# Attention followed by a squared-ReLU feed-forward: single-product weighting of v for the second batch, wider pieces of w_out with their low parts on VectorE, r read later, and the reciprocal moved to the end of its slot

## The chip, the core and the metric

The kernel runs on one core of a Trainium2 chip. The metric is the device time of one execution in microseconds (us), the median of several runs. The engines are TensorE (PE, its weight loads PEld), VectorE (DVE), ScalarE (ACT), GpSimd (POOL) and SyncE (SP), which issues all DMAs here. Each engine takes its instructions strictly in program order, and waits at an instruction until what it needs is there.

## The reference

```python
q_n, k_n = rmsnorm(q, g_q), rmsnorm(k, g_k)          # (8, 12, 448, 64) each
attn = softmax(q_n @ k_n.T / sqrt(64))               # maximum taken off before exp
x = (attn @ v).transpose(0, 2, 1, 3).reshape(3584, 768)
r = np.maximum(x @ w_in, 0.0)                        # w_in (768, 2048)
g = s * (r * r) + b
out = g @ w_out                                      # w_out (2048, 768), out (3584, 768)
```

Inputs are float32, but `w_in` and `w_out` enter with 64 bits per element: the kernel reads them as pairs of 32-bit words and rebuilds a float32 from the words on the chip.

## The kernel before, in words

**Numbers.** A TensorE product in the fast one-pass type (`F32R`) keeps only part of a float32, so a value is split in a high part (an ACT copy to that type) and a low part (what is left, a subtraction), and three products high×high, low×high, high×low stand for one float32 product. The alternative is one product in plain `F32`, which PE runs as two longer instructions.

**Attention (lines 209 to 657).** There are 8 batches of 6 pairs of heads; a pair has 8 slots, one for each head and chunk of 128 keys (`W = 8`), so a batch is 48 slots and there are 384. A loop over slots writes out the order of every engine by hand. In slot `s_` it issues: the transposed scores `st` of slot `s_` (two matmuls, lines 405 and 408), a third of the filler matmuls, the ACT copy `ah` of the exponents of slot `s_-1` (`split_e`), the exponent of slot `s_`, the jobs that a table `jobs` holds for this slot, the scores `sh` of slot `s_+10` for the row maximum (line 367), the low part `al` of slot `s_-1` (`split_e_lo`, line 445, DVE), the maximum (line 378, DVE), the conversion of a piece of `w_in` (`convert`), and the weighting of v for slot `s_-2` (`weigh`, line 464). The jobs of a pair whose first slot is `s0` include: reading v (`load_v`), splitting v in high and low (`split_v`, ACT and POOL), norms and scaling of q and k (DVE line 330, POOL line 329), their low parts (POOL, lines 351 and 352), taking the sums of the softmax out (`gather`, a DMA into `zt`, at `s0+7` and `s0+11`), `divide` step 0 at `s0+13` (add 1e-9 and reciprocal of `zt` on DVE, lines 489 and 490), step 1 (store), step 2 (broadcast load into `zb`) and step 3 at `s0+18` (POOL, line 505, gives `u`). In the slots 11, 12 and 13 of the next batch `split_x` splits the `u` in high and low parts `x` (ACT 513, DVE 514), two pairs in each slot.

In the first batch (pairs `p < NP = 6`) the exponents stay float32 and `weigh` is one float32 product per slot with `vf` (v beside a block of ones, for the sums); from the second batch on, `weigh` is three F32R products (two in every fourth slot, where the low part shares the tile `ah`).

**First matrix of the feed-forward.** From slot 61 on the filler matmuls are `ffn_in` of the batch before (line 180): 16 units of 18 matmuls per batch, 6 per slot. ACT takes each unit's relu out of PSUM (`rectify`, line 197), and SP stores it (`r_d`). Pieces of `w_in` (512 columns, 24 of them) are read and converted in slots -18 to about 94 (`PACE`).

**The row between the matrices (lines 660 to 746, the "w_out row" below).** After attention, the last batch's 16 units of `ffn_in` are left. A loop `m = 0..19` issues a unit (for `m < 16`) and the conversion of three pieces of `w_out` (128 rows × 256 columns, 48 in all): four DVE operations per piece (lines 125, 128, 130, 133), an ACT square (126), and four rounds later an ACT copy to the high part `woh` (136) and a POOL subtraction to the low part `wol` (139), since `woh` and `wol` lie where the quarters of `w_in` lay. The relu of unit `m` stands in round `m` on ACT, between these. In rounds 7 to 12 the squares of the first three tiles of 128 tokens are made (`squares`: ACT 682, DVE 683, then ACT 687 gives `gh`, DVE 688 `gl`); their `r` is read from memory ahead of the loop. The eight PSUM banks are handed out in the order in which they come free.

**Second matrix.** `ffn_out` (line 700): for a tile of 128 tokens 16×3×2 matmuls of 384 columns. The first three tiles share each quarter of `w_out` as it becomes ready; then come tiles 3 to 27, one at a time. These matmuls, and all DMAs of this part, stand in an order that the framework's scheduler chooses.

## Time and profile before

| | us |
|---|---|
| three timed runs | 1546.6, 1547.24 (median), 1549.03 |
| the profiled execution, its device time | 1545.13 |
| its span from the first to the last instruction | 1543.3 |

So 1.8 us of the profiled execution lie outside its span, and it is 2.1 us below the median of the timed runs. In the profile a line such as `L445` is a line of the kernel before; a group's row gives busy time, the mean duration of one, and the idle time of the engine ahead of it with what ended that. A row of the timeline gives start, duration, engine, line, operation, tiles and, in brackets, the wait that ended there; a row of the windows gives each engine's busy time and its count of instructions, the granted clock of TensorE as a share of the full one, and the DMA engines' share. TensorE's durations overlap, so its pace is read from start to start.

### The profile page before, as it was taken

What the parts mean: (1) busy time and instruction counts of PE and PEld (TensorE: products, weight loads), DVE (VectorE), ACT (ScalarE), POOL (GpSimd) and SP (SyncE); (2) the same over time, 40 slices, a digit from 0 to 9 for tenths busy, and PEclk for the clock granted to TensorE, in tenths of its full rate; (3) what the DMA queues carried; (4) which work ended last, traced back from release to release, by engine and by line L of the source; (5) the groups of instructions that cost most, each with busy time, mean ns of one, the idle gap of its engine ahead of it and who ended that gap; (6) DMA issues with size and microseconds to landing.
All of it is one profiled execution on the core that took longest, in us unless ns stands there. A gap on an engine that the chain in (4) does not pass through costs nothing. (4 is left out here: it accounts for less than half of the span.)

```text
span 1543.3 us, 21847 instructions
## 1 busy us (share of the span) xinstructions
PE 1459.3 (95%) x7380; PEld 1343.6 (87%) x7380; DVE 892.6 (58%) x1399; ACT 812.5 (53%) x1522; POOL 748.6 (49%) x611
## 2 busy tenths in 40 slices
PE   7886799999999999999999999997899999999998
PEld 6654688899899899899889889996899999999998
DVE  5989998766666766766666664389532222222210
ACT  4766676666666666766766666346342222222210
POOL 6799898777667667667677753135500000000000
PEclk8998899999999999999999999998899999999999
DMA  4477676566566566656666651466243323323300
GB/s 118 133 198 217 183 231 201 161 193 202 159 189 191 173 193 193 183 166 201 189 172 194 188 164 56 125 218 199 82 140 91 97 75 88 101 76 86 103 21 31
DMA packets 218751, 230.86 MB, mean 150 GB/s; under 512 B 72912, under 2 KB 193744, under 8 KB 218640
## 3 DMA queue, kind: packets, MB, share of 16 engines
q1 hardware_dynamic: 218640, 229.47, 50.3%
q8 instruction: 58, 0.95, 0.3%
q14 instruction: 53, 0.43, 0.1%
HBM read 177.21 MB, written 40.84 MB: 141 GB/s over the span
## 5 line engine op out<-in xcount | busy, mean ns | idle before, releaser
L180 PE MATMUL ph<-x,wih 128*128 128x448 f32 x1536 | 493.1, 368 | 0.0
L424 ACT ACTIVATE st<-st 128x448 f32<-128x448 f32 x336 | 176.5, 525 | 261.2 <-PE st L408 244.6
L180 PEld LDWEIGHTS ph<-x,wih 128*128 128x128 f32 x1536 | 290.8, 189 | 24.0 <-issue 0.2
L378 DVE TENSOR_REDUCE nmx<-sh 112x1 fp32r<-112x448 f32 x384 | 237.1, 620 | 126.4 <-PE sh L367 121.1
L180 PE MATMUL ph<-x,wil 128*128 128x448 f32 x768 | 282.2, 367 | 0.0
L700 PE MATMUL po<-woh,gh 128*128 128x384 f32 x896 | 230.9, 337 | 12.5 <-ACT gh L687 7.8
L700 PE MATMUL po<-wol,gh 128*128 128x384 f32 x896 | 230.5, 337 | 4.1 <-POOL wol L139 4.1
L700 PE MATMUL po<-woh,gl 128*128 128x384 f32 x896 | 229.1, 336 | 0.0
L464 PE MATMUL av<-ah,vs 128*128 128x448 f32 x672 | 194.7, 371 | 6.1 <-DVE ah L445 3.2
L445 DVE TENSOR_TENSOR al<-st,ah 128x448 fp32r<-128x448 f32 x252 | 155.5, 617 | 44.6 <-ACT ah L432 26.0
L432 ACT CAST ah<-st 128x448 fp32r<-128x448 f32 x336 | 179.6, 535 | 2.0
L700 PEld LDWEIGHTS po<-woh,gh 128*128 128x128 f32 x896 | 163.4, 189 | 13.9 <-ACT gh L687 8.1
L367 PE MATMUL sh<-ka,qa 128*112 128x448 f32 x384 | 147.8, 387 | 23.0 <-POOL ka L351 8.4
L700 PEld LDWEIGHTS po<-wol,gh 128*128 128x128 f32 x896 | 163.4, 189 | 5.5 <-POOL wol L139 5.5
L700 PEld LDWEIGHTS po<-woh,gl 128*128 128x128 f32 x896 | 162.9, 189 | 0.5 <-DVE gl L688 0.5
L405 PE MATMUL st<-qa,ka 128*128 128x448 f32 (+1 forms) x384 | 159.2, 414 | 0.5 <-ACT e L420 0.5
L180 PEld LDWEIGHTS ph<-x,wil 128*128 128x128 f32 x768 | 145.2, 189 | 11.4
L351 POOL TENSOR_TENSOR ka<-kq,ka 64x448 fp32r<-64x448 f32 x84 | 100.4, 1196 | 108.4 <-ACT ka L348 97.3
L464 PEld LDWEIGHTS av<-ah,vs 128*128 128x128 f32 x672 | 127.5, 191 | 20.3 <-DVE al L445 3.5
L408 PE MATMUL st<-qb,kb 128*128 128x448 f32 (+1 forms) x384 | 142.4, 371 | 0.0
L682 ACT ACTIVATE r<-r 128x2048 f32<-128x2048 f32 x28 | 53.7, 1917 | 168.2 <-DMA r<-r_d 168.2
L367 PEld LDWEIGHTS sh<-ka,qa 128*112 128x112 f32 x384 | 107.7, 281 | 36.0 <-POOL ka L351 9.9
(75 smaller groups left out, 2099.1 us busy)
## 6 DMA issues: line engine op xcount, KB each, us to landing
kq<-in_dram SPq DMA_DIRECT2D x84, 448.0 KB, 4.8
rb<-i_d SPq DMA_DIRECT2D x84, 448.0 KB, 5.5
r_d<-r SPq DMA_DIRECT2D x128, 224.0 KB, 2.0
r<-r_d SPq DMA_DIRECT2D x24, 1024.0 KB, 5.8
raw<-in_dram SPq DMA_DIRECT2D x42, 448.0 KB, 4.7
w64i<-in_dram SPq DMA_DIRECT2D x24, 512.0 KB, 4.8
w64o<-in_dram SPq DMA_DIRECT2D x48, 256.0 KB, 3.1
kb<-ka SPq DMA_DIRECT2D x96, 112.0 KB, 3.4
```

The source lines that it names most:

```text
L180: T.matmul(ph[:, :SEQ], w[:, cc, f0 : f0 + P], xs[b, cc][:, part, :], start=n == 0, stop=n == 3 * NCC - 1,)
L351: G.tensor_tensor(ka[n][D:, a], t[D:, 0], ka[n][D:, a].bitcast(F32), ALU.subtract)
L367: T.matmul(sh[:QC, :SEQ], qa[p % 2][:, a].rearrange("k (p c) -> k c p", c=NQ)[:, c], ka[p % 2][:, a], start=True, stop=True,)
L378: V.tensor_reduce(out=nmxs[p][:, c : c + 1], in_=sh[:QC, :SEQ], op=ALU.max, axis=AX.X, negate=True)
L405: T.matmul(st[:rows, :SEQ], ka[n][:, keys], qa[n][:, q], start=True, stop=False)
L408: T.matmul(st[:rows, :SEQ], kb[n][:, keys], qb[n][:, q], start=False, stop=True,)
L424: S.activation(st[:rows, :SEQ], st[:rows, :SEQ], AF.Exp)
L432: S.copy(ah[:rows], sts[i][0][:rows, :SEQ])
L445: V.tensor_tensor(al, st[:rows, :SEQ], ah[:rows].bitcast(F32), ALU.subtract)
L464: T.matmul(av[:, :SEQ], x, a, start=kc == 0 and m == 0, stop=kc == 3 and m == len(todo) - 1,)
L682: S.activation(r, r, AF.Square)
L700: T.matmul(po[e][0][:, :HALF], x[:, fc, :], w[:, f, e * HALF : (e + 1) * HALF], start=fc == 0 and m == 0, stop=fc == NFC - 1 and m == 2,)
```

## The change

Four things are changed.

1. `NV = 2 * NP` takes the place of `NP` wherever the choice between one float32 product and three split products is made. Pairs 6 to 11, the second batch, lose `split_v`, `split_e` and `split_e_lo`; their exponent goes to SBUF as float32 on ACT, v is read by two DMAs with two POOL memsets, and `weigh` is one float32 product.
2. `w_out` comes in 32 pieces of 384 columns, two per round `m`, with four buffers for the words from memory (five before), and the low part is subtracted by DVE (`rest=V`), one step after the ACT copy of the high part.
3. The reads of `r` for the first three tiles are issued in rounds 1, 2 and 3 and no longer ahead of the loop, and their squares stand in rounds 6 to 11 (7 to 12 before).
4. The reciprocal of the sums, step 0 of `divide`, is a function of its own, `invert`, which is issued where `convert` is, after the slot's low part and maximum.

```diff
+    NV = 2 * NP
...
-    WO = 256
+    WO = 384
...
-    def load_double(room, dst_hi, dst_lo, src, apart=False):
+    def load_double(room, dst_hi, dst_lo, src, apart=False, rest=None):
...
         S.copy(dst_hi, af)
         if apart:
             yield
-        G.tensor_tensor(dst_lo, af, dst_hi.bitcast(F32), ALU.subtract)
+        (rest or G).tensor_tensor(dst_lo, af, dst_hi.bitcast(F32), ALU.subtract)
...
         def load_v(p):
-            if p < NP:
+            if p < NV:
...
         def exponent(i):
             p, j, kc, rows = chunk(i)
             st, bank = sts[i]
-            if p < NP:
+            if p < NV:
...
         def split_e_lo(i):
             p, j, kc, rows = chunk(i)
-            if p < NP:
+            if p < NV:
                 return
...
+        def invert(p):
+            zt = zts[p]
+            V.tensor_scalar(zt, zt, 1e-9, None, ALU.add)
+            V.reciprocal(zt, zt)
...
+        late = (convert, invert)
...
-            at(s0 - (9 if p >= NP else 5), load_v, p)
-            if p >= NP:
+            at(s0 - (9 if p >= NV else 5), load_v, p)
+            if p >= NV:
                 at(s0 - 3, split_v, p)
-            at(s0 + 13, divide, p, 0)
+            at(s0 + 13, invert, p)
...
                 for f, a in jobs[s_]:
-                    if f is convert:
+                    if f in late:
                         f(*a)
...
-                w = op.tile([P, WO, 2], I32, tag="w64", bufs=5, name=f"w64o{i}")
-                a = op.tile([P, WO], I32, tag="wa", bufs=16, name=f"wao{i}")
-                m = op.tile([P, WO], F32, tag="wm", bufs=3, name=f"wmo{i}")
-                yield load_double((w, lambda a=a: a, m), *part)
+                w = op.tile([P, WO, 2], I32, tag="w64", bufs=4, name=f"w64o{i}")
+                m = op.tile([P, WO], F32, tag="wm", bufs=2, name=f"wmo{i}")
+
+                def words(i=i):
+                    return op.tile([P, WO], I32, tag="wa", bufs=10, name=f"wao{i}")
+
+                yield load_double((w, words, m), *part, apart=True, rest=V)
...
-            todo = list(islice(pieces, 3))
-            for g in chain(todo, first):
+            todo = list(islice(pieces, 2))
+            for g in todo:
                 next(g)
...
+                if m in (1, 2, 3):
+                    next(first[m - 1])
...
-                    if step == 1:
+                    if step == 0:
                         rectify()
                         keep_r()
-                    if step == 2:
                         for g in old:
                             for _ in range(GAP):
                                 next(g)
+                    if step == 2:
+                        for g in old:
+                            next(g)
...
-                if m in (7, 9, 11):
-                    next(first[(m - 7) // 2])
-                if m in (8, 10, 12):
-                    gs.append(next(first[(m - 8) // 2]))
+                if m in (6, 8, 10):
+                    next(first[(m - 6) // 2])
+                if m in (7, 9, 11):
+                    gs.append(next(first[(m - 7) // 2]))
```

The line numbers of the changed kernel are 1 to 12 higher behind these edits. On DVE, in the second batch where `split_x` makes the parts `x` of the first (slots 60 and 61), this stood before: the low parts `al` and `ah` of the exponents, the maxima `nmx`, and `zt` ahead of the scaling of k and q.

```order
L514 TENSOR_TENSOR x_2_1678<-u_1143,x_2_1678 128x448
L514 TENSOR_TENSOR x_3_1681<-u_1292,x_3_1681 128x448
L445 TENSOR_TENSOR ah_1672<-st_1643,ah_1672 64x448
L378 TENSOR_REDUCE nmx_1548<-sh_1684 112x1
L309 TENSOR_REDUCE ssq_1701<-raw_1587 128x14
L489 TENSOR_SCALAR zt_1539<-zt_1539 128x7
L490 RECIPROCAL zt_1539<-zt_1539 128x7
L330 SCALAR_TENSOR_TENSOR kq_1_1608<-kq_1_1608,gqk,rb_1_1610 128x448
L514 TENSOR_TENSOR x_4_1713<-u_1443,x_4_1713 128x448
L514 TENSOR_TENSOR x_5_1716<-u_1626,x_5_1716 128x448
L445 TENSOR_TENSOR al_1723<-st_1669,ah_1698 128x448
L378 TENSOR_REDUCE nmx_1548<-sh_1719 112x1
```

The same place now:

```order
L379 TENSOR_REDUCE nmx_1521<-sh_1615 112x1
L515 TENSOR_TENSOR x_2_1628<-u_1143,x_2_1628 128x448
L515 TENSOR_TENSOR x_3_1631<-u_1290,x_3_1631 128x448
L379 TENSOR_REDUCE nmx_1521<-sh_1634 112x1
L310 TENSOR_REDUCE ssq_1647<-raw_1550 128x14
L331 SCALAR_TENSOR_TENSOR kq_1_1567<-kq_1_1567,gqk,rb_1_1569 128x448
L515 TENSOR_TENSOR x_4_1655<-u_1436,x_4_1655 128x448
L515 TENSOR_TENSOR x_5_1658<-u_1581,x_5_1658 128x448
L379 TENSOR_REDUCE nmx_1521<-sh_1661 112x1
L488 TENSOR_SCALAR zt_1514<-zt_1514 128x7
L489 RECIPROCAL zt_1514<-zt_1514 128x7
```

The subtractions into `al` and `ah` are gone, and the two operations on `zt` stand behind the maximum, at the end of the slot. In the later batches the low parts stay, and `zt` stands behind them in the same way.

In the w_out row, DVE did this before, from the end of one round over the next (here with the squares of a token tile, line 683, between):

```order
L133 SCALAR_TENSOR_TENSOR wao_11279<-wmo_11280,wao_11279 128x256
L133 SCALAR_TENSOR_TENSOR wao_11282<-wmo_11283,wao_11282 128x256
L683 TENSOR_SCALAR r_0_10942<-r_0_10942,sb_s,sb_b 128x2048
L125 TENSOR_SCALAR wao_11333<-w64o_11332 128x256
L125 TENSOR_SCALAR wao_11336<-w64o_11335 128x256
L125 TENSOR_SCALAR wao_11339<-w64o_11338 128x256
L128 SCALAR_TENSOR_TENSOR wao_11333<-w64o_11332,wao_11333 128x256
L128 SCALAR_TENSOR_TENSOR wao_11336<-w64o_11335,wao_11336 128x256
L128 SCALAR_TENSOR_TENSOR wao_11339<-w64o_11338,wao_11339 128x256
L130 SCALAR_TENSOR_TENSOR wao_11333<-w64o_11332,wao_11333 128x256
L130 SCALAR_TENSOR_TENSOR wao_11336<-w64o_11335,wao_11336 128x256
```

And now, in a later round of the same loop (L126, L129, L131 and L134 are the four operations of a piece, L140 the subtraction into `wol`, L689 the squares):

```order
L131 SCALAR_TENSOR_TENSOR wao_11197<-w64o_11143,wao_11197 128x384
L131 SCALAR_TENSOR_TENSOR wao_11200<-w64o_11145,wao_11200 128x384
L140 TENSOR_TENSOR wol_10870<-wao_11007,woh_10869 128x384
L140 TENSOR_TENSOR wol_10870<-wao_11010,woh_10869 128x384
L134 SCALAR_TENSOR_TENSOR wao_11197<-wmo_11144,wao_11197 128x384
L134 SCALAR_TENSOR_TENSOR wao_11200<-wmo_11146,wao_11200 128x384
L689 TENSOR_SCALAR r_2_10877<-r_2_10877,sb_s,sb_b 128x2048
L126 TENSOR_SCALAR wao_11245<-w64o_11191 128x384
L126 TENSOR_SCALAR wao_11248<-w64o_11193 128x384
L129 SCALAR_TENSOR_TENSOR wao_11245<-w64o_11191,wao_11245 128x384
L129 SCALAR_TENSOR_TENSOR wao_11248<-w64o_11193,wao_11248 128x384
```

A round holds two wider pieces in place of three, and two subtractions for the pieces of four rounds earlier, which were POOL's; POOL has nothing left in this row.

SP at the start of the w_out row, before (L121 reads words of `w_out`, L676 reads `r` of a token tile, L207 stores a relu):

```order
L121 DMA w64o_10930<-in_dram 128x512
L121 DMA w64o_10933<-in_dram 128x512
L121 DMA w64o_10936<-in_dram 128x512
L676 DMA r_0_10942<-r_d_74 128x16x128
L676 DMA r_1_10944<-r_d_74 128x16x128
L121 DMA w64o_10967<-in_dram 128x512
L121 DMA w64o_10970<-in_dram 128x512
L121 DMA w64o_10973<-in_dram 128x512
L207 DMA r_d_81<-r_0_10988 128x448
L121 DMA w64o_11016<-in_dram 128x512
L121 DMA w64o_11019<-in_dram 128x512
```

And now (L122, L682, L208):

```order
L122 DMA w64o_10720<-in_dram 128x768
L122 DMA w64o_10722<-in_dram 128x768
L122 DMA w64o_10745<-in_dram 128x768
L122 DMA w64o_10747<-in_dram 128x768
L682 DMA r_0_10791<-r_d_74 128x16x128
L208 DMA r_d_81<-r_0_10757 128x448
L122 DMA w64o_10785<-in_dram 128x768
L122 DMA w64o_10787<-in_dram 128x768
L208 DMA r_d_81<-r_1_10799 128x448
L122 DMA w64o_10827<-in_dram 128x768
L122 DMA w64o_10829<-in_dram 128x768
L682 DMA r_1_10833<-r_d_74 128x16x128
```

Four pieces, those of two rounds, are asked for ahead of the first `r`, and the second `r` stands two rounds further back.

More of the change, by code (lines that the diff above doesn't have):

```diff
@@ L394, in chunk @@
             j, kc = divmod(g, NKC)
-            return p, j, kc, P if kc < 3 or p < NP else REST
+            return p, j, kc, P if kc < 3 or p < NV else REST
         def score_t(i):
@@ L435, in split_e_lo @@
             p, j, kc, rows = chunk(i)
-            if p < NP:
+            if p < NV:
                 return
@@ L455, in weigh @@
             moved = movers.pop(i)
-            if p < NP:
+            if p < NV:
                 of = vrs[p].rearrange("p c u d -> p c (u d)")
@@ L483, in gather @@
             )
+        def invert(p):
+            zt = zts[p]
+            V.tensor_scalar(zt, zt, 1e-9, None, ALU.add)
+            V.reciprocal(zt, zt)
         def divide(p, step):
-            if step == 0:
-                zt = zts.pop(p)
-                V.tensor_scalar(zt, zt, 1e-9, None, ALU.add)
-                V.reciprocal(zt, zt)
-                zts[p] = zt
-            elif step == 1:
+            if step == 1:
                 nc.sync.dma_start(z_d[p].rearrange("j (p c) -> (j p) c", c=TILES), zts.pop(p))
@@ L645, in attention_then_relu2_ffn @@
                 for f, a in jobs[s_]:
-                    if f is convert:
+                    if f in late:
                         f(*a)
@@ L716, in attention_then_relu2_ffn @@
         pieces = pieces()
-        n = 3 * NFC // NS
+        later_by = NFC // NS
         with tc.manual_schedule(engines=ORDERED - {ENGINE.SP}):
             waiting = []
-            todo = list(islice(pieces, 3))
-            for g in chain(todo, first):
+            todo = list(islice(pieces, 2))
+            for g in todo:
                 next(g)
-            for m in range(NFC + NFC // NS):
+            for m in range(NFC + later_by):
                 if m < NFC:
@@ L726, in attention_then_relu2_ffn @@
                         pass
-                now, todo = todo, list(islice(pieces, 3))
+                now, todo = todo, list(islice(pieces, 2))
                 for g in todo:
                     next(g)
-                old = waiting[:3] if m >= NFC // NS else []
+                if m in (1, 2, 3):
+                    next(first[m - 1])
+                old = waiting[:2] if m >= later_by else []
                 waiting = waiting[len(old) :]
@@ L774 @@
     vs = v.reshape(n, 2, s, d)[:, :, keys].transpose(0, 3, 2, 1, 4)
-    vs[: n // b, : p // 2, 3] = 0
+    vs[: 2 * n // b, : p // 2, 3] = 0
     g = _np.stack([_np.tile(_np.asarray(inputs[x]), 2) for x in ("g_q", "g_k")], 1)
```

## Prediction

> **What bounds the kernel now.** The page first: engines' totals, and the span in 40 slices.
>
> ```profile
> PE 1459.3 (95%) x7380; PEld 1343.6 (87%) x7380; DVE 892.6 (58%) x1399; ACT 812.5 (53%) x1522; POOL 748.6 (49%) x611
> PE   7886799999999999999999999997899999999998
> PEclk8998899999999999999999999998899999999999
> ```
>
> TensorE bounds nearly everything. It has holes in two places, the first six slices (to about 240 us) and around slice 28 (1040 to 1100 us), and there the granted clock dips too. An edit can pay only in a hole or by shorter TensorE work. So I asked for windows cut at what the program does: slots 48 to 60 (the second batch ahead of the filler), 61 to 95 (with it), the third and fourth batch, then the w_out row from the last matmul of the first matrix, and the rest.
>
> ```profile
> 126.00:160.90 34.90, 23.79 (x77) 17.06 (x76) 33.85 (x47) 23.72 (x49) 33.80 (x26) 0.83 0.71 211
> 160.90:260.50 99.60, 88.13 (x413) 77.64 (x412) 96.35 (x141) 68.55 (x140) 86.23 (x60) 0.97 0.67 201
> 260.50:379.00 118.50, 115.63 (x566) 105.32 (x565) 80.21 (x132) 81.29 (x167) 82.51 (x66) 1.00 0.63 187
> 379.00:499.00 120.00, 117.15 (x565) 106.47 (x564) 80.38 (x132) 81.27 (x167) 82.39 (x67) 0.99 0.61 182
> 1049.20:1104.00 54.80, 38.21 (x180) 34.94 (x180) 46.22 (x91) 31.13 (x66) 34.72 (x28) 0.81 0.60 176
> 1104.00:1543.30 439.30, 435.24 (x2511) 434.92 (x2509) 103.70 (x76) 102.56 (x76) 3.83 (x6) 1.00 0.28 81
> ```
>
> The columns are length, busy time (with counts) of PE, PEld, DVE, ACT and POOL, granted clock, DMA share, GB/s. In slots 48 to 60 DVE and POOL are both busy 97% of the time; in 61 to 95 DVE is (96.35 of 99.6), POOL 87%. From the third batch on PE is. In the w_out row 180 matmuls take 54.8 us; at the pace of the last window (439.3 / 2511 = 0.175 us each) they need 31.5. **23.3 us are lost in that row**, the largest single loss.
>
> **The second batch.** The price of one float32 product comes from a slot of the first batch, PE's timeline:
>
> ```profile
> 95.51 0.37 PE L367 MATMUL sh<-ka,qa 128*112 128x448 f32 x1
> 95.71 0.91 PE L464 MATMUL av<-e,vf 128*128 128x448 f32 x2
> 96.12 0.71 PE L405 MATMUL st<-qa,ka 128*128 128x448 f32 x1
> 96.67 0.36 PE L408 MATMUL st<-qb,kb 128*128 128x448 f32 x1
> 96.87 0.47 PE L367 MATMUL sh<-ka,qa 128*112 128x448 f32 x1
> ```
>
> The slot takes 1.36 us (95.51 to 96.87). One fast matmul takes about 0.20 (96.67 to 96.87); less three of them (sh, st twice), the product costs 0.75. The split form has 11 matmuls in four slots, 2.75 × 0.20 = 0.56. So PE pays 0.19 more per slot. A slot of the third batch takes (118.5 − 2.8 of holes, below) / 48 = 2.41 us, so a PE-bound slot with filler becomes 2.60. What leaves DVE in the filler's part, and, from the waits of the whole span, what PE waits for at `av`:
>
> ```profile
> L445 DVE TENSOR_TENSOR al<-st,ah 128x448 fp32r<-128x448 f32 x27 | 16.6, 614 | 0.6 <-ACT ah L432 0.6
> L445 DVE TENSOR_TENSOR ah<-st,ah 64x448 fp32r<-64x448 f32 x9 | 5.6, 618 | 0.6 <-ACT ah L432 0.4
> PE av L464 <- DVE al L445: 34.2, 22, 3.3
> ```
>
> 22.2 us of DVE's 96.35 go, which leaves 74 in 35 slots, 2.1 each, under PE's 2.60. PE becomes the bound: 35 × 2.60 = 91 where 99.6 were. I leave 1.6 us for stalls that stay (x parts at the start, POOL at 86 of 91): **7 us gained**, between 3 and 8.6. In slots 48 to 60 taking from DVE alone does not help, as POOL is as full:
>
> ```profile
> L298 POOL TENSOR_TENSOR vs<-vr,vs 128x512 fp32r<-128x512 f32 x42 | 54.7, 1303 | 109.1 <-issue 97.4 <-ACT vs L297 10.7 <-POOL qb L352 1.0
> L295 POOL MEMSET vs<- 128x256 f32 x4 | 1.1, 304 | 0.0
> L282 POOL MEMSET vf<- 128x256 f32 x6 | 1.9, 313 | 0.2
> ```
>
> For each of two pairs there, one split (1.30) and two memsets (0.61) go, and a memset of 0.31 and a smaller one come, some 0.45: 2 × 1.46 = 2.9 us. That is the estimate: **3 us**, from 0 (if POOL's inputs are late) to 6 (if the 97% of both come from waiting for each other). ACT loses an operation per slot, which is worth nothing at 24 of 34.9 us. Two DMAs per v in place of one go through SP 7 slots before use: hidden by those slots, or a wait of 1 or 2 us once per pair.
>
> **The reciprocal.** Every later batch has the same two holes at its split of x, the second largest here:
>
> ```profile
> 295.89 0.16 DVE L489 TENSOR_SCALAR zt<-zt 128x7 f32<-128x7 f32 x1
> 296.09 0.20 DVE L490 RECIPROCAL zt<-zt 128x7 f32<-128x7 f32 x1
> 296.21 1.35 DVE L330 SCALAR_TENSOR_TENSOR kq<-kq,gqk,rb 128x448 f32<-128x448 f32 x1
> 297.48 1.17 DVE L514 TENSOR_TENSOR x<-u,x 128x448 fp32r<-128x448 f32 x2
> 298.57 0.61 DVE L445 TENSOR_TENSOR al<-st,ah 128x448 fp32r<-128x448 f32 x1
> 292.16 0.47 PE L464 MATMUL av<-al,vs 128*128 128x448 f32 x1 [0.96 <-DVE al L445]
> 299.24 0.47 PE L464 MATMUL av<-al,vs 128*128 128x448 f32 x1 [1.88 <-DVE al L445]
> 417.74 0.60 PE L464 MATMUL av<-al,vs 128*128 128x448 f32 x1 [1.86 <-DVE al L445]
> 418.00:421.30 3.30, 3.30 (x10) 2.67 (x10) 2.12 (x5) 1.44 (x4) 1.35 (x2) 0.50 0.20 40
> ```
>
> `zt` holds up the low part, and so PE, by 0.32 us (295.89 to 296.21) in six batches: 1.9 us (0 if L330 then waits for POOL as long, 6 if it gets in ahead). What is queued behind it: only the next slot's work, which now waits if `zt`'s DMA is late; nothing PE needs for two slots. After the hole at 417.74 the clock is 0.50 for 3.3 us, in which 10 matmuls run where 16 would at 0.20 us each: that is why the batch from 379 takes 120.0 us and the one from 260.5, with the same hole, 118.5. If 1.55 us of hole no longer bring that dip, and I suppose it in half of three such batches, another 2.3 us come: **4 us**, 0 to 8. The Trainium skill (TensorE: Matmul & The Clock Gate, "What's actually happening") has the clock halved only after an idle window of about 3.4 us; the trace halves it after 1.86 us. By the page these dips have nothing to do with the holes, and the sum would be 2.3 us smaller.
>
> **The w_out row.** What PE waits for there:
>
> ```profile
> 1051.05 0.44 PE L700 MATMUL po<-woh,gh 128*128 128x384 f32 x1 [1.50 <-ACT r L197]
> 1063.07 0.69 PE L700 MATMUL po<-woh,gh 128*128 128x384 f32 x1 [7.76 <-ACT gh L687]
> 1065.32 0.69 PE L700 MATMUL po<-woh,gh 128*128 128x384 f32 x1 [1.56 <-ACT r L197]
> 1098.92 1.37 PE L700 MATMUL po<-wol,gh 128*128 128x384 f32 x2 [3.64 <-POOL wol L139]
> 1012.64 1.09 DVE L128 SCALAR_TENSOR_TENSOR wao<-w64o,wao 128x256 int32<-128x256 int32 x3
> 1019.99 0.49 DVE L125 TENSOR_SCALAR wao<-w64o 128x256 int32<-128x256 int32 x2
> 1071.73 1.33 DVE L683 TENSOR_SCALAR r<-r,sb_s,sb_b 128x2048 f32<-128x2048 f32 x1
> 1076.62 2.28 DVE L688 TENSOR_TENSOR gl<-r,gh 128x2048 fp32r<-128x2048 f32 x1
> 1081.21 2.71 DVE L128 SCALAR_TENSOR_TENSOR wao<-w64o,wao 128x256 int32<-128x256 int32 x3
> 1096.52 1.08 DVE L133 SCALAR_TENSOR_TENSOR wao<-wmo,wao 128x256 f32<-128x256 f32 x3
> ```
>
> The relus and `gh` stand in the rounds' order on ACT, and the rounds run at DVE's pace: round 4 starts at 1020.0, round 15 ends at 1097.6, 6.5 us a round. Of that, DVE's own work at its best is 3.6 (three operations of 256 columns in 1.09, so about 0.34 each, nine of them, and 0.2 for each L125); the same three take 2.71 while POOL subtracts. Now a round has, at 384 columns, between 0.34 for 256 and 0.60 for 512 in the attention part, 0.47 for each of six operations, 0.30 for each L125, and 0.47 for each of two subtractions (297.48: two of 448 columns in 1.09): 4.4 us, with nothing of POOL's beside it. Round 4 I take to start at 1020 as before: the first rounds wait for memory, and through round 4 the same words and the same two `r` are read; earlier or later by 3. The two `r` are wanted in rounds 6 and 8, so their later place on SP is hidden by four rounds; without these the squares would hold ACT, and each late us would be paid in full. Unit 11's relu, which frees the bank of the second token tile's second half, runs near the start of round 11: 1020 + 7 × 4.4 + three squares (3 × 1.33) + two `gl` (2 × 2.28) = 1059. PE wants it 24 matmuls after 1049.2, at 1053.4: a wait of 5.5, in place of 1.50 + 7.76 + 1.56, and half clock for a window (1.7) or two behind it. The last low parts come at 1020 + 12 × 4.4 + 10.4 + 4 = 1087, and PE reaches that quarter after 216 matmuls, at 1049.2 + 37.8 + 8 = 1095: the 3.64 at 1098.92 and its slow stretch go. Lost in all 8 to 9 of 23.3: **14 us gained**, 5 (round 11 at 1068) to 18.
>
> **Sum.** 7 + 3 + 4 + 14 = 28 us off the profiled 1545.1 gives 1517; its run lies 2.1 below the median of the timed runs, so off 1547.2: **1519 us**.
>
> **Rivals.**
> - *POOL keeps the second batch.* It is at 86 of 99.6 us with the filler and still full ahead of it, and if its waits pass to PE, only 3 of the 10 us come: 1526. For it: 33.80 of 34.9. Against: PE's longest waits at `av` end with DVE's `al` (34.2 us, 22 times, holes of the later batches among them). Chance 0.15.
> - *Memory holds the w_out row.* A round reads 786 KB (128 × 768 × 8 bytes) and stores 229 KB (128 × 448 × 4); at the 176 GB/s of the window 1049 to 1104 that is 5.8 us, not 4.4, and each `r` (128 × 2048 × 4 bytes) adds 6. Round 11 then starts at 1020 + 40.6 + 6 = 1067, and the last quarter at about 1110, so this row gains nothing or loses up to 6: 1533 to 1539. Against: other windows reach 211 GB/s. Chance 0.13.
> - *DVE is too full for the low parts* (the slower side). If a subtraction costs DVE what it cost POOL in this row, 1282 ns, and the 6.5 us round stays, a round (squares included, as in the 6.5) takes 6.5 + 2.6 = 9.0, the last low parts come at 1020 + 108 + 4 = 1132, 37 us after PE wants them: 1547 − 14 + 22 = 1555. It turns the whole to slower from a round of about 8.4 us. Against: DVE's stretching stands beside POOL's work, which goes. Chance 0.05. The Trainium skill (Perfetto Trace Analysis, "Optimizing Scalar/DVE Operations") speaks for this side: with DVE saturated, giving work to Scalar or GpSimd may help, and this takes it back. It adds that the two share a read port; the 2.71 against 1.09 agrees with that.
> - *More*: the holes close wholly (6 + 4.6) and the half clock with them, 1511. Chance 0.07.
>
> ```profile
> L139 POOL TENSOR_TENSOR wol<-wao,woh 128x256 fp32r<-128x256 f32 x28 | 35.1, 1282 | 23.1 <-ACT woh L136 12.6 <-DVE wao L128 5.4 <-DVE gl L688 5.2
> ```
>
> **The numbers.** The forecast has 0.60. Its own bounds add to 8 (1539) and 40 (1507); not all go one way, so 1510 to 1534 holds most of it. The rivals of POOL and of more lie inside; memory's lies at the upper edge, DVE's outside: 1510 to 1535 leaves out about 0.2. A difference of 0.2%, 3.1 us, is about what a measurement can tell from no change. Faster 0.93, within 0.2% 0.03 (memory and POOL together), slower 0.04.
>
> **What would show it.** Windows of the second batch: slots 61 to 95 in 91 to 94 us with PE full and DVE near 75; slots 48 to 60 in 29 to 34. Batches of 118.5 where 120.0 were. In the w_out row, rounds of 4.4 us, no DVE operation of 2.7, the first wait of PE for a relu near 5 us and none for `wol`. I am wrong if PE still waits for `al`-like DVE work in the second batch, if rounds take 6 us or more, or if the second holes stay at 1.88.

## The result and the profile after

| | before | after |
|---|---|---|
| timed runs, median (lowest to highest), us | 1547.2 (1546.6 to 1549.03) | **1497.95** (1496.81 to 1499.82) |
| after / before, 95% interval | | 0.9681 [0.9664, 0.9698] |
| profiled execution, its span, us | 1545.13, 1543.3 | 1498.21, 1496.4 |

The kernel is 49 us faster; 1519 was forecast, with a range of 1510 to 1535. Direction and places were right, the size was not. The page of the kernel after, the engines' totals, and TensorE's two rows of the span in 40 slices:

```profile
PE 1449.9 (97%) x7344; PEld 1328.8 (89%) x7344; DVE 872.9 (58%) x1319; ACT 785.3 (52%) x1436; POOL 691.3 (46%) x569
PE   7987999999999999999999999999999999999998
PEclk9999999999999999999999999999999999999999
```

The dip around slice 28 is gone altogether; the first slices stay thin. The windows of the kernel after, cut at the same places of the program as those of before (slots 48 to 60, 61 to 95, third and fourth batch, the first 180 matmuls of the second matrix, the rest):

```profile
123.40:149.40 26.00, 20.52 (x68) 13.22 (x66) 22.61 (x35) 13.80 (x29) 25.07 (x20) 0.93 0.79 203
149.40:247.20 97.80, 94.11 (x387) 74.98 (x386) 84.77 (x107) 55.47 (x109) 83.92 (x69) 0.97 0.77 223
247.20:365.20 118.00, 116.14 (x565) 105.19 (x564) 81.06 (x131) 81.21 (x166) 85.03 (x69) 1.00 0.65 189
365.20:482.70 117.50, 115.64 (x565) 105.33 (x564) 82.38 (x132) 81.27 (x167) 83.98 (x67) 1.00 0.64 187
1025.80:1057.30 31.50, 31.35 (x181) 31.03 (x180) 31.23 (x66) 20.12 (x36) 0.00 (x0) 1.00 0.67 202
1057.30:1496.40 439.10, 435.03 (x2510) 434.71 (x2508) 106.47 (x79) 102.57 (x76) 0.00 (x0) 1.00 0.28 81
```

180 matmuls now take 31.5 us where they took 54.8: the w_out row loses nothing. What TensorE still waits for at `av`, and the two holes left in a later batch, from the waits and from PE's timeline:

```profile
PE av L465 <- DVE al L446: 11.0, 12, 1.0
```

```profile
396.88 0.48 PE L465 MATMUL av<-al,vs 128*128 128x448 f32 x1 [0.96 <-DVE al L446]
402.96 0.47 PE L465 MATMUL av<-al,vs 128*128 128x448 f32 x1 [0.87 <-DVE al L446]
```

34.2 us in 22 waits became 11.0 in 12: two holes in each of six batches, the second 0.87 us where it was 1.88, and the granted clock stays at 1.00 behind them.

Where the time went, by the start of TensorE's `st` of slots 48, 61, 96 and 383 and its first `po`, in the profiled execution of each kernel (us; `e1` to `e13` are the experiments below). From slot 383 to the first `po` it is 77.4 in every one.

| kernel | to slot 48 | 48 to 60 | 61 to 95 | 96 to 383 | first `po` to end |
|---|---|---|---|---|---|
| before | 126.0 | 34.9 | 99.6 | 711.3 | 494.1 |
| after | 123.4 | 26.0 | 97.9 | 701.1 | 470.6 |
| e1, second batch alone | 123.4 | 27.7 | 96.2 | 713.5 | 490.3 |
| e2, reciprocal alone | 121.0 | 35.8 | 97.9 | 700.6 | 490.4 |
| e3, w_out row alone | 125.6 | 38.0 | 97.9 | 712.8 | 471.0 |
| e12, x late as well | 125.0 | 27.6 | 93.9 | 689.6 | 471.0 |

After against before: 2.6 + 8.9 + 1.7 + 10.2 + 23.5 = 46.9 us. Predicted were 0, 3, 7, 4 and 14.

### The profile page after: what moved, and what is told of

It is laid out like the page before. It is cut to its first block, busy times and chain, and to the rows that moved or that the text cites. A ratio compares the mean times of both kernels' runs of the same rounds, so it can differ in the third digit from the quotient of the medians.

```text
span 1496.4 us, 21405 instructions
## 1 busy us (share of the span) xinstructions
PE 1449.9 (97%) x7344; PEld 1328.8 (89%) x7344; DVE 872.9 (58%) x1319; ACT 785.3 (52%) x1436; POOL 691.3 (46%) x569
## 4 chain that ended last, share of the span: by engine, by line
PE 85%; DVE 7%; POOL 3%; DMA 3%; issue 2%; ACT 1%; SPq 0%; DVEq 0%; POOLq 0%; ACTq 0%
PE po L706 31%; PE ph L181 26%; PE av L465 13%; PE st L406 4%; PE st L409 4%; PE sh L368 4%; DVE x L515 2%; PE warmth L272 1%; DMA w64o<-in_dram 1%; DMA rb<-i_d 1%; POOL ri L314 1%; DVE wao L129 1%; DVE nmx L379 1%; DVE wao L131 1%; DVE wao L134 1%
## 5 line engine op out<-in xcount | busy, mean ns | idle before, releaser
L181 PE MATMUL ph<-x,wil 128*128 128x448 f32 x768 | 294.6, 384 | 0.0
L425 ACT ACTIVATE st<-st 128x448 f32<-128x448 f32 (+1 forms) x288 | 151.1, 525 | 220.9 <-PE st L409 204.3
L465 PE MATMUL av<-ah,vs 128*128 128x448 f32 x576 | 164.3, 366 | 0.1
L433 ACT CAST ah<-st 128x448 fp32r<-128x448 f32 (+1 forms) x288 | 154.1, 535 | 1.8
L446 DVE TENSOR_TENSOR al<-st,ah 128x448 fp32r<-128x448 f32 x216 | 132.1, 611 | 36.3 <-ACT ah L433 21.7
L689 DVE TENSOR_SCALAR r<-r,sb_s,sb_b 128x2048 f32<-128x2048 f32 x28 | 37.6, 1346 | 172.4 <-ACT r L688 172.4
```

Of the source, the lines that this page charges most:

```text
L181: T.matmul(ph[:, :SEQ], w[:, cc, f0 : f0 + P], xs[b, cc][:, part, :], start=n == 0, stop=n == 3 * NCC - 1,)
L425: S.activation(st[:rows, :SEQ], st[:rows, :SEQ], AF.Exp)
L433: S.copy(ah[:rows], sts[i][0][:rows, :SEQ])
L446: V.tensor_tensor(al, st[:rows, :SEQ], ah[:rows].bitcast(F32), ALU.subtract)
L465: T.matmul(av[:, :SEQ], x, a, start=kc == 0 and m == 0, stop=kc == 3 and m == len(todo) - 1,)
```

## The experiments

All are timed beside the kernel before (median 1545.9 to 1548.2 in these groups).

| kernel | median, us | ratio to before, 95% |
|---|---|---|
| e1, before + second batch | 1530.79 | 0.9896 [0.9877, 0.9916] |
| e2, before + reciprocal | 1527.45 | 0.9877 [0.9859, 0.9896] |
| e3, before + w_out row | 1524.38 | 0.9852 [0.9837, 0.9866] |
| e4, after, low parts on POOL | 1514.11 | 0.9787 [0.9771, 0.9803] |
| e5, after, r ahead of the loop | 1497.85 | 0.9688 [0.967, 0.9706] |
| e6, after, 256 columns | 1499.97 | 0.9697 [0.9683, 0.971] |
| e7, after, `zt` ahead of `x` | 1509.52 | 0.9761 [0.9748, 0.9775] |
| e8, after, first `x` early | 1498.80 | 0.969 [0.9677, 0.9704] |
| e9, after, third batch in float32 | 1503.90 | 0.9717 [0.9703, 0.9732] |
| e10, after, sums a slot later | 1520.79 | 0.9824 [0.9809, 0.9838] |
| e11, e5 and e6 together | 1501.27 | 0.9701 [0.9685, 0.9717] |
| e12, after, `x` late | **1485.73** | 0.9597 [0.9583, 0.9612] |
| e13, e11 with five word buffers | 1502.35 | 0.9713 [0.9696, 0.9731] |

### The three parts alone: e1, e2, e3

Each is the kernel before with one part of the change's diff. e1, with its `p < NV` for `p < NP` wherever v, the exponents and `weigh` are concerned:

```diff
+    NV = 2 * NP
```

e2, the reciprocal and nothing else:

```diff
-            at(s0 + 13, divide, p, 0)
+            at(s0 + 13, invert, p)
...
+        late = (convert, invert)
```

e3, the part from line 660 on as changed:

```diff
-    WO = 256
+    WO = 384
...
+                yield load_double((w, words, m), *part, apart=True, rest=V)
...
+                if m in (1, 2, 3):
+                    next(first[m - 1])
```

> The kernel before with the second batch's float32 products alone. Theory (the parts add, each stretch gains what the traces' slot starts say): slots 0 to 95 gain 13.3 us as in the whole change (2.6 by slot 48, 8.9 in slots 48 to 60, 1.8 in 61 to 95), the later batches keep their second hole of about 1.88 us and the half clock behind some of them: 1534, 1532 to 1536. Rival (the prediction's terms, 3 + 7): 1537, with slots 48 to 60 near 32 us and 61 to 95 near 92. Rival (the moved reciprocal gives part of what the first 96 slots gained): 1538 to 1541.

> The kernel before with the reciprocal moved to the end of its slot and nothing else. Theory (the scaling of k and q now starts ahead of POOL's, which shrinks it from 1.35 to 0.68 us, beside the 0.32 us of the two operations on the sums): the second hole of the batches goes from 1.88 to 0.9, six times 1.0 = 6 us, and the half clock behind three of them goes, 4.5 us: 1537, 1535 to 1539. Rival (the prediction's term): 0.32 us a batch and half of the dips, 4 us: 1543. Rival (the holes shrink only together with the second batch's change): 1547, no difference.

> The kernel before with the w_out row alone changed (pieces of 384 columns, low parts by DVE, r read later). Theory: the row stands by itself, no hole of TensorE is left in it: 23.4 us gained, 1524, 1522 to 1526. Rival (the prediction's term): 14 us, 1533, with a wait of about 5 us for a relu.

They gained 17.4, 20.7 and 23.8 us of the medians: e3 came as expected, e1 was 3 us and e2 10 us faster than expected. The rows of PE in the fourth batch, of e1 and then of e2:

```profile
406.86 0.47 PE L465 MATMUL av<-al,vs 128*128 128x448 f32 x1 [1.86 <-DVE al L446]
```

```profile
409.93 0.47 PE L464 MATMUL av<-al,vs 128*128 128x448 f32 x1 [0.87 <-DVE al L445]
```

So the holes and dips of the later batches belong to the reciprocal alone: e2 has all of that gain (711.3 to 700.6), e1 none of it. Slots 48 to 95 belong to the second batch alone: 10.6 us in e1, 0.8 in e2. (How much this stretch varies by itself: 133.7 to 136.0 us in before, e2 and e3, and 121.3 to 125.4 in the kernels with the changed second batch, e10 with its 133.4 apart.) The w_out row stands by itself in e3 (494.1 to 471.0).

The three sum to more than the whole: 14.7 + 20.3 + 20.5 = 55.5 us of the profiled executions against 46.9, and 61.9 against 49.2 by the medians. By the table, 7.1 of the 8.6 lie behind the first `po`: e1 and e2 take 3.8 and 3.7 us less there than before, although nothing in that part was changed in them; another 5.4 lie ahead of slot 48, and the stretches between give 3.9 the other way. In e1 TensorE's wait for `gh` is 5.1 us where it was 7.76. So the row as it was before loses between 19 and 23 us in kernels in which nothing of it was changed; why, these runs do not show. The stretch to slot 48 varies between 120.6 and 126.2 us over the kernels run. The 2.6 us of the first stretch are therefore not shown to be the change's.

### What the reciprocal's place does: e7

```diff
-        late = (convert, invert)
+        late = (convert,)
...
+        for listed in jobs.values():
+            listed.sort(key=lambda job: {invert: 1, split_x: 2}.get(job[0], 0))
```

> The changed kernel with the two operations on the sums issued between the scaling of k and q and the parts x: behind the scaling, but again ahead of the low part and the maximum. Theory (what counts is that the scaling starts ahead of POOL's): the scaling stays at 0.68 us, the second hole of the later batches is 0.87 + 0.32 = 1.2 us in place of 0.87: 6 x 0.32 = 2 us slower, 1500. Rival (the position behind the low part and the maximum is what shrank the hole, by any price): the hole is 1.9 again, with half clock behind some: 1504 to 1508.

It is 11.6 us slower, more than the whole later-batch gain; the expected price of 2 us was wrong, and the rival's hole was right (its time was 1.5 us too short). First the kernel before, the fourth batch, POOL and DVE at the scaling of k and q (`kq`):

```profile
414.43 1.15 POOL L329 TENSOR_TENSOR kq<-kq,rb 128x448 f32<-128x448 f32 x1
414.71 1.34 DVE L330 SCALAR_TENSOR_TENSOR kq<-kq,gqk,rb 128x448 f32<-128x448 f32 x1
```

The kernel after, the same place:

```profile
400.65 2.71 POOL L330 TENSOR_TENSOR kq<-kq,rb 128x448 f32<-128x448 f32 x1
400.62 0.68 DVE L331 SCALAR_TENSOR_TENSOR kq<-kq,gqk,rb 128x448 f32<-128x448 f32 x1
401.21 1.15 DVE L515 TENSOR_TENSOR x<-u,x 128x448 fp32r<-128x448 f32 x2
402.29 0.61 DVE L446 TENSOR_TENSOR al<-st,ah 128x448 fp32r<-128x448 f32 x1
```

And e7:

```profile
402.26 1.66 POOL L330 TENSOR_TENSOR kq<-kq,rb 128x448 f32<-128x448 f32 x1
402.23 0.68 DVE L331 SCALAR_TENSOR_TENSOR kq<-kq,gqk,rb 128x448 f32<-128x448 f32 x1
402.82 1.13 DVE L488 TENSOR_SCALAR zt<-zt 128x7 f32<-128x7 f32 x1
404.11 1.14 DVE L515 TENSOR_TENSOR x<-u,x 128x448 fp32r<-128x448 f32 x2
```

Before, POOL began 0.28 us ahead of DVE, and DVE's scaling took 1.34 us. After, DVE begins 0.03 us ahead: its scaling takes 0.68, and POOL's operation waits, not only for that one but for the two on `x` behind it, and takes 2.71 where it took 1.15. In e7 the scaling is first as well (0.68), but then `zt`, seven columns that took 0.16 us, takes 1.13: POOL got in between, and the loss is back, one instruction further on. The hole is 2.1 us again, with the clock at half behind it in three of six batches. So two things make the gain: the 0.32 us are off the path, and they let DVE start first with nothing behind it that lets POOL in before the low part is done. The Trainium skill (SBUF — State Buffer, "SBUF: two separate sides") says that DVE and POOL share a pair of ports as an exclusive lock, taken by whichever starts first, for the whole instruction, by DVE for operations with two SBUF inputs or in a two-port mode. The 0.28 and 0.03 us, and the 0.66 that they turn, agree; the 2.71 us go further, as POOL here stays out over three DVE instructions. Whether `zt`, with one SBUF input, runs in such a mode, no run here shows; its 1.13 us say that it waits all the same.

Who starts first by the trace is not all that counts. In the kernel after, each of the six later batches also has this pair, a little further on:

```profile
407.64 1.93 POOL L353 TENSOR_TENSOR qb<-kq,qa 64x448 fp32r<-64x448 f32 x1
407.88 0.68 DVE L331 SCALAR_TENSOR_TENSOR kq<-kq,gqk,rb 128x448 f32<-128x448 f32 x1
```

POOL begins 0.24 us ahead, and yet it is POOL that waits, and DVE's 0.68 us are not stretched. Here DVE comes from a maximum, in the kernel before it came from `zt`. So starts that lie a few tenths of a microsecond apart do not tell the outcome by themselves; no run here separates whether the scaling won because it came 0.31 us sooner against POOL or because the short `zt` no longer stands in front of it.

### The w_out row: e4, e5, e6, e11, e13

e4 puts the low parts back on POOL, all else as changed:

```diff
-                yield load_double((w, words, m), *part, apart=True, rest=V)
+                yield load_double((w, words, m), *part, apart=True)
```

> The changed kernel with the low parts of w_out back on POOL; width, order and r as changed. Theory (DVE's operations with two SBUF inputs wait for POOL's running one): rounds 5 to 12 take 5.5 to 6.5 us where they take 4.3, though DVE has 0.94 us less to do in each; relu 11 comes 6 to 12 us late: 1506 to 1514. Rival (width and fewer operations are what shortened the round; POOL's place is free): a round of 3.4 to 4.3 us, no hole, 1498, same.

16.2 us slower, and 15.6 in the row (486.2 for 470.6). The groups of DVE from the start of round 4 to the start of round 15, first of the kernel after:

```profile
L129 DVE SCALAR_TENSOR_TENSOR wao<-w64o,wao 128x384 int32<-128x384 int32 x23 | 11.8, 554 | 0.0
L131 DVE SCALAR_TENSOR_TENSOR wao<-w64o,wao 128x384 int32<-128x384 int32 x22 | 11.3, 554 | 0.0
L140 DVE TENSOR_TENSOR wol<-wao,woh 128x384 fp32r<-128x384 f32 x22 | 11.3, 554 | 0.0
L126 DVE TENSOR_SCALAR wao<-w64o 128x384 int32<-128x384 int32 x24 | 7.7, 358 | 2.5 <-DMA w64o<-in_dram 2.5
```

and of e4, with POOL's group, one of its instructions, and PE's waits:

```profile
L126 DVE TENSOR_SCALAR wao<-w64o 128x384 int32<-128x384 int32 x23 | 15.5, 703 | 5.1 <-POOL wol L140 2.7 <-DMA w64o<-in_dram 2.4
L129 DVE SCALAR_TENSOR_TENSOR wao<-w64o,wao 128x384 int32<-128x384 int32 x22 | 14.4, 692 | 0.0
L140 POOL TENSOR_TENSOR wol<-wao,woh 128x384 fp32r<-128x384 f32 x22 | 40.2, 1854 | 48.8 <-DMA w64o<-in_dram 26.7 <-ACT woh L137 17.3 <-DVE wao L129 4.8
```

```profile
1035.55 6.18 POOL L140 TENSOR_TENSOR wol<-wao,woh 128x384 fp32r<-128x384 f32 x1 [4.26 <-ACT woh L137]
```

```profile
PE po L706 <- ACT r L198: 12.6, 2, 7.7
```

Work taken from DVE makes DVE slower: 22 subtractions (11.3 us) go, but `L126` goes from 358 to 703 ns and each of the others rises, and TensorE waits 12.6 us for relus whose rounds come later. One POOL subtraction stands for 6.18 us beside a busy DVE.

e5 reads r ahead of the loop as before, e6 has 256 columns (three pieces a round, six buffers for the words), e11 has both, and e13 has both with five buffers, as before the change. Of the change to the row e13 keeps the low parts on DVE and the places of relu, subtraction and squares in the rounds.

```diff
-            for g in todo:
+            for g in chain(todo, first):
                 next(g)
...
-                if m in (1, 2, 3):
-                    next(first[m - 1])
```

```diff
-    WO = 384
+    WO = 256
...
-                w = op.tile([P, WO, 2], I32, tag="w64", bufs=4, name=f"w64o{i}")
-                m = op.tile([P, WO], F32, tag="wm", bufs=2, name=f"wmo{i}")
+                w = op.tile([P, WO, 2], I32, tag="w64", bufs=6, name=f"w64o{i}")
+                m = op.tile([P, WO], F32, tag="wm", bufs=3, name=f"wmo{i}")
...
-                    return op.tile([P, WO], I32, tag="wa", bufs=10, name=f"wao{i}")
+                    return op.tile([P, WO], I32, tag="wa", bufs=15, name=f"wao{i}")
...
-                now, todo = todo, list(islice(pieces, 2))
+                now, todo = todo, list(islice(pieces, 3))
...
-                old = waiting[:2] if m >= later_by else []
+                old = waiting[:3] if m >= later_by else []
```

and e13 against e11:

```diff
-                w = op.tile([P, WO, 2], I32, tag="w64", bufs=6, name=f"w64o{i}")
+                w = op.tile([P, WO, 2], I32, tag="w64", bufs=5, name=f"w64o{i}")
```

> The changed kernel with the reads of r issued ahead of the loop, as before; all else as changed. Theory (the prediction failed at 'round 4 starts as before': reading r later is what brought round 4 from 27.0 to 20.8 us behind the row's start): round 4 starts at about 26 to 27 us again, unit 11's relu comes 5 to 6 us after TensorE wants it, with half clock behind it: 1504 to 1507. Rival (the wider pieces and the four buffers brought round 4 forward, r's place is worth nothing): 1498, no hole, round 4 at 21 us.

> The changed kernel with pieces of 256 columns, three per round, six buffers for the words (the same bytes); low parts on DVE and r read late as changed. Theory (per-operation cost): a round is three times 0.20 and 0.34 x 3, and three subtractions of 0.34, 5.9 us less nothing, at best 4.7 by DVE's own durations: relu 11 comes 7 x 0.4 = 3 us later than now, a wait of about 2.5 and half clock for a window: 1501 to 1504. Rival (memory sets the round, or there is slack enough): 1498, no hole. Rival (short rows of memory are read slower, round 4 is as late as before): 1506 or more.

> The changed kernel with both at once: pieces of 256 columns, and r read ahead of the loop. Of the change to the w_out row only the low parts on DVE and the places on ACT are left. Theory (the prediction's step 'round 4 starts as before' fails by two halves, the rounds ahead of it being 0.6 to 1 us shorter each and r 2.9 us out of the way; either alone leaves a wait of about 1 us): round 4 starts at 26 to 27 us behind the row's start, unit 11's relu at 66 to 68 where TensorE wants it at 60: a wait of 5 to 7 and half clock behind it, 7 to 11 us slower, 1505 to 1509. Rival (each half costs about 1 us and they add): 1500.

> The kernel with 256 columns and r ahead of the loop, and besides five buffers for the words in place of six, as in the kernel before: of the change to the row only the low parts on DVE and the places on ACT are left, and the rounds are read exactly as before. Theory (the buffers that hold two whole rounds are the third thing that brought round 4 forward: with five, the third piece of each round waited about 0.6 us): round 4 at 27.0 us behind the row's start as before, not 24.9; rounds 1 to 3 of 4.4 us; unit 11's relu at about 67, a wait of 4 us where it was 2.1, and half clock: 1504. Rival (the buffers don't matter): round 4 at 25, 1501, same as with six.

Measured from the first read of words of the row (993.03 before, 969.92 after), when DVE's round 4 starts and ACT's relu of unit 11, and the stretch from the first `po` to the end, which is 470.6 to 471.6 in all kernels with the changed row:

| | round 4 | relu 11 | first `po` | to the end |
|---|---|---|---|---|
| before | 27.0 | 71.7 | 56.2 | 494.1 |
| after | 20.8 | 59.1 | 55.9 | 470.6 |
| e5, r ahead | 23.7 | 61.3 | 56.2 | 471.8 |
| e6, 256 columns | 21.4 | 62.2 | 56.0 | 472.6 |
| e11, both | 24.9 | 64.7 | 56.1 | 474.2 |
| e13, both, five buffers | 26.5 | 69.5 | 55.9 | 475.8 |

r's place, width and buffers each brought some of the 6.2 us: with r and width put back 2.1 remain, with the buffers too 0.5. e5 is at the edge of what the row varies by. The times that the theories of e5, e6 and e11 gave were too long, by at least 6, 1 and 4 us.

The 6.2 us lie between rounds 0 and 1. The first operation of round 1 on DVE, in before, after and e13:

```profile
1006.72 0.29 DVE L125 TENSOR_SCALAR wao<-w64o 128x256 int32<-128x256 int32 x1 [5.32 <-DMA w64o<-in_dram]
```

```profile
977.13 0.62 DVE L126 TENSOR_SCALAR wao<-w64o 128x384 int32<-128x384 int32 x2
```

```profile
982.09 0.29 DVE L126 TENSOR_SCALAR wao<-w64o 128x256 int32<-128x256 int32 x1 [5.50 <-DMA w64o<-in_dram]
```

With two `r` ahead of the words of round 1, DVE waits 5.0 to 5.5 us for these words (4.97 in e5); after, it does not wait. Rounds 0 and 1 begin 10.8 us apart before, 10.3 in e13, 9.0 in e5, 5.0 in e6 and 4.0 after, while rounds 1 to 4 take 13.3 us before and 13.6 after. In e5 they take 11.2, so that of the 5 us that r costs ahead of round 1 a good 2 come back where r is out of the way. The buffers show in DVE's timeline of e13, where the third piece of each round waits for its words, as it does in before:

```profile
987.78 0.29 DVE L126 TENSOR_SCALAR wao<-w64o 128x256 int32<-128x256 int32 x1 [0.68 <-DMA w64o<-in_dram]
992.24 0.29 DVE L126 TENSOR_SCALAR wao<-w64o 128x256 int32<-128x256 int32 x1 [0.73 <-DMA w64o<-in_dram]
```

But even e13, with round 4 where the prediction had it and relu 11 later still, loses only 5.2 us of the row. Its time was expected at 1504 with a wait of 4 us; it has no wait above 1.64 and no half clock (e11 has one dip of 3.4 us, behind its wait of 2.10). The rows of PE in e5, e11 and e13 that wait for a relu, in that order:

```profile
1027.52 0.44 PE L706 MATMUL po<-woh,gh 128*128 128x384 f32 x1 [1.11 <-ACT r L198]
```

```profile
1034.04 0.57 PE L706 MATMUL po<-woh,gh 128*128 128x384 f32 x1 [2.10 <-ACT r L198]
```

```profile
1026.09 0.45 PE L706 MATMUL po<-woh,gh 128*128 128x384 f32 x1 [0.88 <-ACT r L198]
1039.03 0.44 PE L706 MATMUL po<-woh,gh 128*128 128x384 f32 x1 [1.64 <-ACT r L198]
```

The reason lies in TensorE's order, which the scheduler writes anew for each kernel. The first 72 matmuls of the second matrix by the accumulator that they write (1 and 2 are the halves of the first token tile, 3 and 4 of the second, 5 and 6 of the third):

```
before 121212121212121212121212343434343434343434343434121212121212121212121212
e4     121212121212121212121212343434343434343434343434565656565656565656565656
after  121212121212121212121212343434343434343434343434121255121212555555555512
e11    121212121212121212121212333333333333121244444444444412121212121212121212
e13    121212121212121212121212333333333333121212121212121212333444444444444121
```

Accumulator 4 lies in the bank that unit 11's relu frees. Before, after and in e4 it is wanted as matmul 26, in e11 as matmul 41, in e13 as matmul 58: the work is put around the late bank. The relu of e13 begins at 69.5 and the matmul starts at 70.0; as matmul 26, some 61 us behind the row's start, it would have waited 8 to 9 us, which is an estimate from 0.175 us a matmul. No run has the one order with the other's times. e4 has the strict order, so part of its 15.6 us may be the order's, not the port's; this was not separated.

### The second batch, and a price: e8 and e9

```diff
-                at(W * NP * (b + 1) + START - 2 + k_, split_x, b, k_)
+                early = (8, 4, 0)[k_] if b == 0 else 0
+                at(W * NP * (b + 1) + START - 2 + k_ - early, split_x, b, k_)
```

> The changed kernel with the first batch's parts x split in slots 51, 56 and 61 in place of 59, 60 and 61 (their u are there). Theory (the waits of 0.74 and 2.85 us in slots 61 to 64, and the half clock from 157.1 to 164.0 behind them, come from four x parts in two slots, of which the second pair takes 4.2 us beside POOL): those waits go, 6 us gained, 1492, 1490 to 1495. Rival (POOL, busy 25.1 of 26.0 us in slots 48 to 60, bounds the whole stretch, and what is taken out of slots 59 and 60 is paid in 51 and 56): 1498, same.

No difference. Slots 61 to 95 take 91.7 us, 6 less, and slots 48 to 60 take 31.3, 5 more. What the waits at slot 61 cost is paid earlier in full, as the rival had it; POOL is busy 25.07 of 26.0 us there in the kernel after.

e9 takes the third batch in as well:

```diff
-    NV = 2 * NP
+    NV = 3 * NP
...
-    vs[: 2 * n // b, : p // 2, 3] = 0
+    vs[: 3 * n // b, : p // 2, 3] = 0
```

> The changed kernel with the third batch's v (slots 96 to 143) in float32 products too. Theory (TensorE is the bound there and pays 0.19 us more per slot, as the prediction worked out from a slot of the first batch): 48 x 0.19 = 9.1 us more for the products, less that batch's holes of 0.96 + 0.87, which end with the low parts gone: 7 us slower, the batch at 125 where it takes 118.0: 1505. Rival (what freed DVE and POOL in the second batch frees them here as well): 1498 or less.

6.0 us slower. The window of the third batch of e9:

```profile
247.80:371.00 123.20, 123.20 (x530) 100.43 (x529) 50.10 (x84) 57.63 (x113) 82.67 (x74) 1.00 0.62 179
```

TensorE is without a hole, 123.2 / 48 = 2.57 us a slot. Without its holes the split form took (118.0 − 1.8) / 48 = 2.42, so a float32 product costs 0.15 us more per slot, not 0.19. It pays only where it frees something that bounds.

### Two more places for DVE's work: e10 and e12

```diff
-                at(s0 - 28, norm, p)
+                at(s0 - 27, norm, p)
```

> The changed kernel with the squares of q and k and their sums (ACT line 305, DVE line 310, 1.08 us) one slot later, so that the sums no longer share a slot with the scaling of k and q and two parts x. Theory (the hole of 0.87 us is DVE's work of one slot too many: low part, maximum, sums, scaling and two parts x, 4.0 us against TensorE's 2.41): the hole of 0.87 goes in six batches, 5.2 us gained, 1493. Rival (the scaling then starts 1.0 us sooner and meets POOL's operation on vs in place of that on kq, and waits for it): the hole stays or grows, 1498 to 1503.

22.8 us slower, more than either expected. The hole became 1.82, with half clock behind it in three batches. DVE and POOL of e10 in the fourth batch:

```profile
412.81 2.08 POOL L299 TENSOR_TENSOR vs<-vr,vs 128x512 fp32r<-128x512 f32 x1 [3.58 <-issue]
413.05 0.68 DVE L331 SCALAR_TENSOR_TENSOR kq<-kq,gqk,rb 128x448 f32<-128x448 f32 x1
414.01 2.83 DVE L515 TENSOR_TENSOR x<-u,x 128x448 fp32r<-128x448 f32 x2 [0.29 <-ACT x L514]
414.85 1.52 POOL L330 TENSOR_TENSOR kq<-kq,rb 128x448 f32<-128x448 f32 x1
```

The square on ACT moved along with the sums, and lies ahead of ACT's `x` now; DVE waits 0.29 us for it, POOL's `vs` gets in, which the scaling had held up, and then its `kq`, and the two `x` take 2.83 us in place of 1.15. The scaling met POOL's `vs`, as the rival had it, but it was POOL that waited; what was held up on DVE were the `x`. Slots 61 to 95 lost 5.8 us besides; why was not followed.

```diff
                 S.copy(x[:, 0, :], u)
-                V.tensor_tensor(x[:, 1, :], u, x[:, 0, :].bitcast(F32), ALU.subtract)
+                halves.append((u, x))
...
+        def split_x_lo(n):
+            for _ in range(n):
+                u, x = halves.pop(0)
+                V.tensor_tensor(x[:, 1, :], u, x[:, 0, :].bitcast(F32), ALU.subtract)
...
-        late = (convert, invert)
+        late = (convert, invert, split_x_lo)
...
+                at(W * NP * (b + 1) + START - 2 + k_, split_x_lo, 2)
```

> The changed kernel with DVE's two low parts of x behind the slot's low part of the exponents and its maximum, where the reciprocal stands now; ACT's high parts as they were. Theory (the low part of the exponents is what TensorE waits for, and x has two slots before TensorE reads it): the holes of 0.96 and 0.87 us shrink to less than 0.5 each, 6 to 10 us gained, 1488 to 1492. Rival (DVE's work in slots 59 to 61 is too much by itself, so the holes move one slot later, into the low part or into the filler's wait for x): 1497 to 1500.

1485.73: 12.2 us faster than the kernel after, 4.0% faster than before, and the best version here (1488 to 1492 was expected). The fourth batch of e12, its window and its only hole:

```profile
362.50:478.10 115.60, 115.20 (x566) 105.36 (x566) 80.41 (x132) 81.23 (x167) 85.08 (x67) 1.00 0.65 190
398.36 0.48 PE L465 MATMUL av<-al,vs 128*128 128x448 f32 x1 [0.40 <-DVE al L446]
```

DVE does the same work in these slots; only what TensorE waits for comes first. Slots 96 to 383 take 689.6 us where they took 701.1.

## Why the prediction was wrong, point by point

**The second batch: the sum was right, its parts were not.** 3 + 7 = 10 us were predicted for slots 48 to 95, 10.6 came, and e1 shows that they belong to this edit. But slots 48 to 60 gave 8.9 (the bound "if the 97% of both come from waiting for each other" was 6), and 61 to 95 gave 1.7. TensorE's pace was right: behind the first four slots 2.57 us a slot where 2.60 was predicted. The 1.6 us left for stalls were too few. Cut at slot 65, where POOL's backlog is worked off, the two stretches gain 4.9 and 5.8: the cut at slot 61 divided one queue. In slots 48 to 60 POOL has three each of `kq`, `ka`, `qb` and `u` where it had four, 16.3 us for 23.4; that work now stands behind slot 61. The 3 us rested on a misreading besides, "each of two pairs there": POOL's rows of before have one split (1.3 us) and two memsets (0.6) in slots 48 to 60, the next split comes at slot 61. So that the sum came out at 10 is in part luck. The rival that POOL keeps the second batch did not come.

**The reciprocal: a mis-sized term.** The step was "0.32 us ... 6 if it gets in ahead", and I took the 0.32, six times. It got in ahead, by 0.03 us; the hole shrank by 1.0, the 0.32 and the 0.66 that DVE's scaling no longer waits. Of the dips I supposed half to go; all three went. 6 × 1.0 + 3 × 1.5 = 10.5; 10.2 us came where 4 were predicted and 8 was the bound, and e2 gives 10.7 without the rest of the change. That the place and not the mere length matters is shown by e7.

**The w_out row: two steps failed.** The first is "Round 4 I take to start at 1020 as before", earlier or later by 3. It came 6.2 us earlier against the row's start, because I took the same words and the same two r as the same time, though the profile of before has DVE wait 5.32 us at round 1, for words that are asked for behind these two r: r's later place and the wider pieces were priced behind round 4 only, and four buffers for two pieces a round not at all, though five for three pieces left a wait of 0.6 us in each of the early rounds of before. With that alone, the relu at 1059 becomes 1053, when TensorE wanted it, and the row's whole 23.3 us come. The second is "PE wants it 24 matmuls after 1049.2": e13, with round 4 as predicted and relu 11 at 69.5 us against the 66 of the prediction, loses 5.2 us where I had 8 to 9, since the order of TensorE was written anew around the late bank. What lay between held: rounds of 4.29 us against 4.4, no DVE operation stretched by POOL, no wait for `wol`. The main cause was also right: e13 still gains 18.3 of the 23.5 us, and e4, with POOL's subtractions back, only 7.9. How much of that is the new places of the relus on ACT and TensorE's new order, and not the low parts on DVE, was not separated. (Two small slips of the sums change nothing: the 10.4 us for three squares and three `gl` should be 10.8, and 2.75 × 0.20 is 0.55.)

**The rivals.** Memory did not hold the row from round 4 on: rounds of 4.29 us stand in a window of 202 GB/s. Ahead of round 4 it did, as the 5.32 us show. DVE was not too full for the low parts: 31.23 us busy of 31.5, with the whole row as fast as TensorE. "More" came in part; its price, 6 + 4.6, was near what the reciprocal gave alone.

**The clock.** Holes of 1.81 to 2.30 us in the later batches were followed by 3.4 us at half clock in 17 of 30 cases (before, e1, e3, e7, e10); holes of 0.86 to 0.97 in none of 106 (after, e2, e4, e5, e6, e8, e9, e11, e13). The 1.5 us of such a dip belong to the hole's price, at about even odds. Where the hole falls tells 28 of the 30 cases: in every trace here all changes of the granted clock lie on a grid of 3.413 us (in before the three dips begin at 417.92, 656.86 and 895.79, 70 steps apart each). In all 17 cases one step of the grid held at least 1.81 us of the hole, and the dip filled the next step. In 11 of the other 13 the grid cut the hole so that no step held more than 1.75 us of it; in two a step held 1.86 and 1.90 and no dip came. The rule of the Trainium skill (TensorE: Matmul & The Clock Gate, "What's actually happening") that it takes an idle window of 3.4 us fits the length of the dips, but not these holes, of which the shortest that brought one is 1.81 us.

## What to carry to other kernels

Where DVE and POOL both work on SBUF, price an instruction by which of the two gets in first and by what stands in front of it and behind it, not by its length: a seven-column operation moved by half a slot was worth 10 us here, and giving work from DVE to POOL slowed DVE down. Put first in a slot what the bounding engine waits for, and everything with slack behind it. Before a wait is priced, read the bounding engine's new order too, and count buffers against what one round reads: both can move the moment at which a result is wanted or there.

## What was not expected of the hardware

- A POOL operation that comes in behind DVE's waits through several DVE operations, not one: 2.71 us for 1.15 in the kernel after (0.03 us behind), 6.18 us in e4 for one of 384 columns that has a mean of 1.85.
- It can wait even when it begins 0.24 us ahead: 1.93 us beside a scaling of 0.68 that came from a maximum, six times in the kernel after.
- A DVE operation on 128 × 7 elements can take 1.13 us in place of 0.16 when POOL is in (e7).
- A hole of half the length brings no half clock at all, 0 of 106, where the double brought it in 17 of 30, each time with at least 1.81 us of it in one step of a 3.413 us grid.
